# Retention and mixture kernel on one core: GpSimd's two products cut into halves, and the first batch begun in another order

## Chip, cores and metric

The kernel runs on one core of one Trainium2 chip. The metric is the device time of one execution in microseconds (us); lower is better. Of the core's engines, TensorE (PE) multiplies matrices, VectorE (DVE), ScalarE (ACT) and GpSimd (POOL) work element by element, SyncE (SP) issues most of the transfers from memory. PEld in a view is PE's loading of weights.

## What is computed

Three steps follow each other, for 8 batches of 576 rows. Cut to what matters:

```python
# 1: retention with a decay per head, no softmax; q, k, v: 8 batches, 8 heads, 576 rows, 64 wide
x = ((q @ k.T / 8) * gamma ** (i - j), lower triangle) @ v
# 2: four attention experts, two picked for each row by a gate
logits = x @ w_gate
out = sum over picked experts e of weight * softmax(causal(x@wq[e] @ (x@wk[e]).T / 8)) @ (x@wv[e]) @ wo[e]
# 3: phases, mixing over the rows (tokens), a channel product
theta = x @ w_theta; y = w_tok_r @ (x*cos(theta)) + w_tok_i @ (x*sin(theta)); u = x + y
return u + relu(u @ w_ch)
```

## The kernel before, in words

Retention goes through each batch in five chunks of 128 rows, the last one of 64 (`ROWS`). A chunk is `n` = 2 halves of 64 rows (the last chunk has one). For a chunk c, `loads` (L113) brings `kt` (queries and keys, 512 KB) and `kv` (keys and values in row order, 512 KB) through SP, and has POOL make `vp` (L122), the values scaled by the decay `gam`. `ret_scores` (L137) are 16 products for `sm`; `ret_state` (L153) adds one half's keys times `vp` to a running sum `pS` and ACT copies it to a tile `S` (L156); `ret_values` (L166, L173) sums `sm` times `vp` and `S` times queries in `px`, DVE scales that by `gt` to `xt` (L183), ACT rounds it to `xh` (L185), and POOL takes the remainder `xl` (L186). `ret_step(b, c, next)` interleaves on PE the second state of chunk c, the scores of the next chunk and the values of chunk c, and ends with the next chunk's first state.

A product with rounded and remainder parts is three matmuls: `xh` by `WH`, `xl` by `WH`, `xh` by `WL` (`mm3`, L101 to L103). `WH` and `WL` are made from the loaded weights `wst` by `split` (ACT L106, DVE L107). `proj_v` (L249, 12 matmuls, "v0" to "v4" in `work`) projects one chunk, and takes its four products with `xh` and `WH`, four with `xh` and `WL`, four with `xl` last; `proj_qk` ("k00", "q00", "k01") projects rows 0 to 287 or 288 to 575, 12 matmuls with `mm3`. A projected key is copied by four DMAs, `KK<-KN` (L227). `at_scores` (L311) begins the attention of a batch.

The order on PE is the order of the code (`manual_schedule`), that on the other engines a scheduler's, which may put POOL's `vp` of a later chunk ahead of an `xl`; each engine and each queue then runs strictly in that order. The tiles `kt` and `kv` have three buffers each (`LDB`), `vp` three (`VPB`): `ret_values` of chunk c calls `loads` for the chunk three further on, whose transfer waits until the buffer is free. SP issues no transfer while an earlier one in its list waits.

The program begins with 50 matmuls on a zeroed tile (`WARM`, L393), the loads of chunks 0 and 1, `g0` (from which DVE makes `gt`, L408), the four tiles of `w1`, and chunk 2. For batch 0 the code then goes `ret_step` 0, `ret_step` 1 (between the splits of the weights), v0, `ret_step` 2, v1, `ret_step` 3, v2, k00, `ret_step` 4, q00, v3, k01, v4: the projection of a chunk stands one `ret_step` behind it. From batch 1 on the same steps are spread over the attention units of the batch before (`SLOTS`). After all attention the token and channel products of step 3 follow, where POOL has little to do.

Of the kernel before, what the change touches and what calls it, by code (L numbers as in the profile page):

```python
# [10 lines left out]
F32 = mybir.dt.float32  # L11
# [9 lines left out]
B, H, S, D = 8, 8, 576, 64  # L21
E, DM = 4, 512
C = 128
NCH = 5
ROWS = [128, 128, 128, 128, 64]
# [11 lines left out]
LDB = 3  # L37
# [8 lines left out]
         ("v0", "R3"), ("v1", ""), ("v2 k00", "R4"), ("q00", "R5"), ("v3 k01 v4 g", "")]  # L46
PTV = (0,)
WARM = 50
WB = 7
JOBS = (58, 75)  # L50

# [10 lines left out]
def tile_kernel(ctx: ExitStack, tc: tile.TileContext, qk, kv, w1, wo, wot, wd, cst, out):  # L62
    nc = tc.nc
    consts = ctx.enter_context(tc.tile_pool(name="consts", bufs=1))

    def pool(name, **kw):
        return tc.alloc_tile_pool(name=name, bufs=1, **kw)
# [13 lines left out]
    ps1 = pool("ps1", space=PSUM)  # L81
# [4 lines left out]
    tri = att.tile([128, 64], F32, name="tri")  # L86
    gam = att.tile([128, NCH, 2, 4], F32, name="gam")
# [7 lines left out]
    gt = ret.tile([128, 4, S], F32, name="gt")  # L95
# [14 lines left out]
    MARK = {}  # L110
    QKT, KVT, XT, PSS, VP, SM, PX = {}, {}, {}, {}, {}, {}, {}

    def loads(b, c):  # L113
        R = ROWS[c]
        o = c * 1024
        t = ret.tile([128, 8, R], F32, name="kt", bufs=LDB, padded_shape=[128, 8, 128])
        nc.sync.dma_start(t, qk[b, :, o:o + 8 * R].rearrange("p (h r) -> p h r", h=8))
        n = R // 64
        u = ret.tile([128, 2, 2, 256], F32, name="kv", bufs=LDB)
        nc.sync.dma_start(u[:, :n], kv[b, c, :, :n * 512].rearrange("r (j a d) -> r j a d", j=n, a=2))  # L120
        vp = ret.tile([128, 2, 4, D], F32, name="vp", bufs=VPB)
        MARK["pool"] = nc.gpsimd.tensor_mul(vp[:, :n], u[:, :n, 1, :].rearrange("p j (h d) -> p j h d", h=4),  # L122
                                            gam[:, c, :n, :, None].to_broadcast([128, n, 4, D]))
        QKT[b, c], KVT[b, c], VP[b, c] = t, u, vp

    def half(x):
        return slice(x * 64, x * 64 + 64)

    def ret_scores(b, c):

        n = ROWS[c] // 64
        t = QKT[b, c]
        ps = ps1.tile([128, n, 4, 64], F32, name="w", bufs=WB, padded_shape=[128, 2, 4, 64])
        for j in range(n):
# [9 lines left out]
    def ret_state(b, k):  # L144

        c, j = divmod(k, 2)
        u, vp = KVT[b, c], VP[b, c]
        if k == 0:
            PSS[b] = ps1.tile([128, 4, D], F32, name="pS", bufs=1, padded_shape=[128, 4, 128])
        pS = PSS[b]  # L150
        for x in range(4):
            for s in range(2):
                nc.tensor.matmul(pS[half(s), x, :], u[half(s), j, 0, x * D:x * D + D], vp[half(s), j, x, :],  # L153
                                 start=k == 0 and x == 0, stop=False, skip_group_check=True)
            yield
        nc.scalar.activation(SB[(k + 1) % 4], pS, AF.Copy)  # L156

    def ret_values(b, c):

        R = ROWS[c]  # L160
        t, vp, sm = QKT[b, c], VP[b, c], SM.pop((b, c))
        px = ps1.tile([128, 4, R], F32, name="w", bufs=WB, padded_shape=[128, 4, 128])
        for j in range(R // 64):
            for x in range(4):
                for s in range(2):
                    nc.tensor.matmul(px[half(1 - s), x, half(j)], vp[half(s), j, x, :], sm[half(s), j, x, :],  # L166
                                     start=j == 0 and x == 0, stop=False, skip_group_check=True)
                yield
        for j in range(R // 64):
            k = 2 * c + j  # L170
            for x in range(4 if k else 0):
                for s in range(2):
                    nc.tensor.matmul(px[half(1 - s), x, half(j)], SB[k % 4][half(s), x, :], t[half(s), x, half(j)],  # L173
                                     start=False, stop=False, skip_group_check=True)
                yield
        for x in (QKT, KVT, VP):
            x.pop((b, c))
        cs = slice(c * C, c * C + R)
        if c == 0:
            XT[b] = (w1p.tile([128, 4, S], F32R, name="xh", bufs=1),  # L180
                     w1p.tile([128, 4, S], F32R, name="xl", bufs=1))
        xt = ret.tile([128, 4, R], F32, name="xt", bufs=2, padded_shape=[128, 4, 128])
        nc.vector.tensor_mul(xt, px, gt[:, :, cs])  # L183
        xh, xl = XT[b]
        nc.scalar.activation(xh[:, :, cs], xt, AF.Copy)  # L185
        nc.gpsimd.tensor_sub(xl[:, :, cs], xt, xh[:, :, cs])  # L186
        nx = (b, c + LDB) if c + LDB < NCH else (b + 1, c + LDB - NCH)
        if nx[0] < B:
            loads(*nx)

    def ret_step(b, c, nx, mid=None):

        diag, off = [], []
        if 0 <= c < NCH - 1:
            diag.append(ret_state(b, 2 * c + 1))
        if nx:
            diag.append(ret_scores(*nx))
        if c >= 0:
            off.append(ret_values(b, c))
        last = nx and nx[1] < NCH - 1  # L200
        off = chain(*off)
        for _, _ in zip_longest(chain(*diag), islice(off, 12) if last and mid else off):
            pass
        if mid:
            mid()
        for _ in zip_longest(ret_state(nx[0], 2 * nx[1]) if last else (), off):
            pass
# [4 lines left out]
    def proj_qk(b, p, t, g):  # L212
# [6 lines left out]
        sl = slice(g * HS, g * HS + HS)  # L219
        ps = ps1.tile([128, HS], F32, name="w", bufs=WB, padded_shape=[128, 512])  # L220
        for kt in range(4):
# [15 lines left out]
    def proj_v(b, c):  # L237
# [7 lines left out]
        cs = slice(c * C, c * C + R)  # L245
        ps = ps1.tile([128, NV], F32, name="w", bufs=WB, padded_shape=[128, 512])
        for x, W in ((xh, WH), (xh, WL), (xl, WH)):
# [32 lines left out]
    def work(b, names):  # L280
        for n in names.split():
            x = b + n.islower()
            if x < B:
                if n in "Gg":
                    gate(x)
                elif n[0] == "T":
                    token_tile(ps1, 0, len(X2))
                elif n[0] == "F":
                    fuse(int(n[1]))
                elif n[0] in "Vv":  # L290
                    proj_v(x, int(n[1]))
                else:
                    proj_qk(x, int(n[1]), int(n[0] in "Kk"), int(n[2]))
# [4 lines left out]
    def at_scores(u):  # L298
# [8 lines left out]
        for i, (j0, j1) in enumerate(parts):  # L307
            ps = [ps1.tile([128, j1 - j0], F32, name="w", bufs=WB, padded_shape=[128, 512]) for _ in range(2)]
            for s in range(2):
# [34 lines left out]
    def at_trans(u):  # L344
# [8 lines left out]
        for s in range(2):  # L353
            PT = PTB[b, p, g][s]
            tp = ps1.tile([128, m + 1, R], F32, name="w", bufs=WB, padded_shape=[128, 4, 128] if R == 128 else [128, 8, 64])
            for j in range(m + 1):
# [31 lines left out]
    w1s = pool("w1s")  # L388
    warm = w1s.tile([128, 128], BF, name="warm")
    nc.vector.memset(warm, 0.0)  # L390
    pw = ps1.tile([128, 128], F32, name="w", bufs=WB, padded_shape=[128, 512])
    for _ in range(WARM):
        nc.tensor.matmul(pw, warm, warm, start=True, stop=True)  # L393
    o = 320
    nc.sync.dma_start(gam, cst[:, o:o + NCH * H].rearrange("p (c j h) -> p c j h", c=NCH, j=2))
    for l in LG:
        nc.gpsimd.memset(l, 0.0)
    for x in SUM + NW:
        nc.gpsimd.memset(x, 1.0)
    loads(0, 0)  # L400
    nc.sync.dma_start(tri, cst[:, 256:320])
    loads(0, 1)
    o += NCH * H
    g0 = w1s.tile([128, 4, 128 + NCH], F32, name="g0")
    nc.sync.dma_start(g0, cst[:, o + 1088 + E * E:].rearrange("p (a t) -> p a t", a=4))
    def make_gt(c):
        R = ROWS[c]
        nc.vector.tensor_mul(gt[:, :, c * C:c * C + R], g0[:, :, :R], g0[:, :, 128 + c, None].to_broadcast([128, 4, R]))  # L408
# [8 lines left out]
    def split_w1(kt):  # L417
        split(WH[:, kt, :], WL[:, kt, :], wst[kt])

    for kt in range(4):  # L420
        load_w1(kt)
    for c in range(2, LDB):
        loads(0, c)
    with tc.issue_after(MARK["pool"].ins):
        nc.gpsimd.dma_start(cm, cst[:, o:o + 1088])
    nc.sync.dma_start(tie, cst[:, o + 1088:o + 1088 + E * E].rearrange("p (a b) -> p a b", a=E))
# [65 lines left out]
    def fuse(p):  # L492
# [2 lines left out]
            mm3(acc, wt[:, 0, p, :], wt[:, 1, p, :], th[:, 0, :], th[:, 1, :], kt == 0, kt == 3)  # L495
        split(MH[:, p, :], ML[:, p, :], acc)

    ret_step(0, -1, (0, 0))
    make_gt(0)
    ret_step(0, 0, (0, 1))  # L500
    make_gt(1)
    for kt in range(4):
        split_w1(kt)
        if kt == 1:
            ret_step(0, 1, (0, 2))
    for c in range(2, NCH):
        make_gt(c)
    w1s.release()
    work(-1, "v0")
    ret_step(0, 2, (0, 3))  # L510
    work(-1, "v1")
    ret_step(0, 3, (0, 4))
    work(-1, "v2 k00")
    ret_step(0, 4, (1, 0))
    work(-1, "q00 v3 k01 v4 g")


    X2, NR, OL = {}, {}, {}
# [84 lines left out]
    for t in range(nu + 1):  # L603
        b, k = divmod(t, 10)
        if b < B - 1:
            more, between, after = *SLOTS[k], ""
        else:
            b = B - 1
# [20 lines left out]
        if b < B - 1:  # L629
            if between[:1] == "R":  # L630
                c = int(between[1])
                x = b + 1
                def mid():
                    for o in outs:
                        at_out(*o)
                    outs.clear()
# [11 lines left out]
        x = t - JOBS[0] if i else t - 2  # L648
# [251 lines left out]
```

## Time and profile before

| what | value |
|---|---|
| median of 3 runs | 901.79 us (897.53 to 903.82) |
| the profiled execution's own time | 901.38 us |
| its span (first to last instruction) | 899.6 us |
| PE busy | 864.2 us (96%) |
| DVE, ACT, POOL busy | 614.8, 466.0, 219.2 us |
| data moved | 130.29 MB, mean 145 GB/s |

The span is that of one execution on the profiled chip; 1.8 us of the execution's time lie around it. A busy PE is not a PE at its full rate: the table counts a matmul's whole passage, and the clock that it was granted is another column. Times in the views count from the span's start.

### The profile page before, as it was taken

The numbers are of one execution on the slowest core, as the hardware profiler recorded it, in microseconds if no ns is written. First come the engines' busy times: TensorE is split into PE (matmuls) and PEld (weight loads), VectorE is DVE, ScalarE is ACT, GpSimd is POOL, SyncE is SP. The second block draws the span as 40 slices with busy tenths as digits, with TensorE's granted clock in tenths as the row PEclk, the third lists the DMA queues.
The fourth block names the chain that finished last, engine by engine and source line by source line (L and its number), as shares of the span: only waits on it lengthen the run. The fifth ranks groups of instructions, "written<-read, shape, count | busy, mean of one in ns | idle before, by whom it ended". The sixth has DMA issues, their size and how long they took to land.

```text
span 899.6 us, 25474 instructions
## 1 busy us (share of the span) xinstructions
PE 864.2 (96%) x10062; PEld 804.5 (89%) x10062; DVE 614.8 (68%) x1708; ACT 466.0 (52%) x1270; POOL 219.2 (24%) x268
## 2 busy tenths in 40 slices
PE   6998999999899999999999899999999999999998
PEld 5997888889888988988878899999999999999998
DVE  4276677878788786777768947866568764776622
ACT  2375666666666665666657613543345533445320
POOL 3434262551634435252210112000120101201010
PEclk8999999999999999999999989999999999999999
DMA  8757666676666667657795242333525124251311
GB/s 295 212 155 223 152 210 171 182 244 182 189 186 210 202 188 229 164 144 213 181 322 174 33 128 57 65 86 87 136 50 129 38 70 113 36 129 26 83 47 54
DMA packets 146215, 130.29 MB, mean 145 GB/s; under 512 B 83504, under 2 KB 121648, under 8 KB 146096
## 3 DMA queue, kind: packets, MB, share of 16 engines
q1 hardware_dynamic: 145952, 128.39, 51.1%
q8 instruction: 79, 1.29, 0.6%
q0 software_dynamic: 144, 0.28, 0.2%
q14 instruction: 40, 0.33, 0.1%
HBM read 78.03 MB, written 32.00 MB: 122 GB/s over the span
## 4 chain that ended last, share of the span: by engine, by line
PE 78%; DMA 8%; DVE 6%; POOL 3%; ACT 2%; issue 2%; SPq 1%; POOLq 0%; ACTq 0%; DVEq 0%
PE acc L725 22%; PE w L102 10%; PE w L101 10%; PE w L103 9%; DMA kv<-kv 5%; PE w L311 5%; PE w L377 4%; PE w L249 4%; PE w L358 4%; PE pS L153 2%; PE w L725 2%; PE w L137 1%; POOL xl L186 1%; PE w L173 1%; PE acc L101 1%
## 5 line engine op out<-in xcount | busy, mean ns | idle before, releaser
L725 PE MATMUL acc<-TK,zh 128*128 128x288 f32 (+2 forms) x896 | 155.8, 296 | 0.5 <-ACT ob L381 0.5
L725 PEld LDWEIGHTS acc<-TK,zh 128*128 128x128 f32 x896 | 131.9, 189 | 0.8 <-issue 0.6
L319 ACT ACTIVATE P<-P,st 128x128 f32<-128x128 f32 (+4 forms) x160 | 95.6, 598 | 44.0 <-DVE st L314 43.7
L725 PE MATMUL acc<-TK,zl 128*128 128x288 f32 (+1 forms) x448 | 95.8, 295 | 0.0
L741 POOL TENSOR_TENSOR ul<-u,uh 128x576 fp32r<-128x576 f32 x16 | 24.3, 1533 | 285.0 <-ACT uh L740 284.9
L314 DVE CUSTOM_DVE_ANT_0 P<-w,cm 128x128 f32<-128x128 f32 (+4 forms) x160 | 71.9, 476 | 10.7 <-PE w L311 10.3
L102 PE MATMUL w<-xl,WH 128*128 128x288 f32 x256 | 75.9, 296 | 2.9 <-POOL xl L186 2.9
L311 PE MATMUL w<-KK,U 128*64 128x288 f32 (+4 forms) x384 | 76.4, 327 | 0.7 <-DMA KK<-KN 0.7
L101 PE MATMUL w<-xh,WH 128*128 128x288 f32 x256 | 76.1, 297 | 0.6 <-issue 0.6
L103 PE MATMUL w<-xh,WL 128*128 128x288 f32 x256 | 75.4, 295 | 0.0
L725 PEld LDWEIGHTS acc<-TK,zl 128*128 128x128 f32 x448 | 72.3, 189 | 0.0
L106 ACT ACTIVATE zh<-cs 128x512 fp32r<-128x512 f32 x64 | 40.3, 630 | 59.7 <-PE acc L725 42.7
L107 DVE TENSOR_TENSOR zl<-cs,zh 128x512 fp32r<-128x512 f32 x64 | 44.1, 689 | 37.6 <-ACT zh L106 37.0
L576 ACT ACTIVATE cs<-cs,quarter 128x256 f32<-128x256 f32 x72 | 36.4, 506 | 60.1 <-DVE cs L574 57.2
L377 PE MATMUL w<-PT,V 128*64 128x192 f32 (+3 forms) x576 | 56.6, 325 | 6.8 <-DVE PT L363 6.3
L579 DVE SCALAR_TENSOR_TENSOR cs<-cs,x 128x512 f32<-128x512 f32 x72 | 49.3, 687 | 19.6 <-ACT cs L577 18.8
L449 POOL TENSOR_TENSOR r<-r,ex 128x192 f32<-128x192 f32 (+1 forms) x51 | 29.5, 578 | 133.3 <-ACT hl L450 57.2
L311 PEld LDWEIGHTS w<-KK,U 128*128 128x128 f32 (+1 forms) x384 | 54.1, 171 | 6.9 <-issue 2.1
L358 PE MATMUL w<-ident,P 128*128 128x128 f32 (+2 forms) x480 | 58.8, 257 | 0.0
L153 PE MATMUL pS<-vp,kv 64*64 64x64 f32 x1024 | 45.9, 227 | 12.7 <-ACT S L156 9.6
L377 PEld LDWEIGHTS w<-PT,V 128*64 128x64 f32 (+1 forms) x576 | 36.3, 135 | 24.0 <-DVE PT L363 7.1
L122 POOL TENSOR_TENSOR vp<-kv,gam 128x512 f32<-128x512 f32 (+1 forms) x40 | 38.6, 966 | 74.0 <-DMA kv<-kv 59.7
(160 smaller groups left out, 2415.1 us busy)
## 6 DMA issues: line engine op xcount, KB each, us to landing
KK<-KN SPq DMA_DIRECT2D x128, 144.0 KB
kt<-qk SPq DMA_DIRECT2D x32, 512.0 KB
kv<-kv SPq DMA_DIRECT2D x32, 512.0 KB
raw<-wd SPq DMA_DIRECT2D x43, 192.0 KB
xd<-xb SPq DMA_DIRECT2D x126, 64.0 KB
out<-u SPq DMA_DIRECT2D x28, 288.0 KB
u<-xd SPq DMA_DIRECT2D x28, 288.0 KB
td<-hl SPq DMA_DIRECT2D x27, 192.0 KB
```

The costliest lines, as they stand in the source:

```text
L101: nc.tensor.matmul(ps, ah, bh, start=first, stop=False)
L102: nc.tensor.matmul(ps, ah, bl, start=False, stop=False)
L103: nc.tensor.matmul(ps, al, bh, start=False, stop=last)
L107: nc.vector.tensor_sub(l, src, h)
L153: nc.tensor.matmul(pS[half(s), x, :], u[half(s), j, 0, x * D:x * D + D], vp[half(s), j, x, :], start=k == 0 and x == 0, stop=False, skip_g ...
L311: nc.tensor.matmul(ps[s][:R], U[:, s, rs], KK[:, s, x, j0:j1], start=x == 0, stop=x == 1)
L314: MARK["dve"] = nc.vector.tensor_tensor_reduce(Ps[s][:R, j0:j1], ps[s][:R], cm[:R, o + j0:o + j1], 1.0, st[:R, 0, s:s + 1] if i else 3.0e3 ...
L319: MARK["act"] = nc.scalar.activation(Ps[s][:R, :n], Ps[s][:R, :n], AF.Exp, bias=st[:R, last, s:s + 1], scale=-1.0, accum_out=SUM[p][:R, m, ...
L358: nc.tensor.transpose(tp[:w, j, :], Ps[s][:R, j * C:j * C + w], ident[:R, :R])
L377: nc.tensor.matmul(po[s * 64:s * 64 + 64, c0:], V[:ROWS[j], j, 2 * p + s, :], v, start=j == 0, stop=j == last, skip_group_check=True)
L579: nc.vector.scalar_tensor_tensor(z, cs, -1.0, x2[:, None, ds].to_broadcast([128, 2, 256]), op0=OP.mult, op1=OP.mult)
L725: nc.tensor.matmul(acc[d][j], A[:, dc], TK[:, kt, W, t0:t1], start=q == 0 and n == 0, stop=q == 8 and n == 2)
```

## The change

Two things. First, POOL's `vp` is made by one instruction for each half of 64 rows, and `xl` by one instruction for each two of the four slices of the model's width, everywhere. Second, the beginning: `g0` and then chunk 0 alone are loaded ahead of the weights, chunks 1 and 2 after them; the `vp` of later chunks of batch 0 is made where the code says (`scale_v`) and no longer within `loads`; all of `gt` is made first; `ret_step` 0 computes no scores of chunk 1; the weights are split after chunk 0's `xt`; 40 more matmuls on the zeroed tile follow (`WARM2`), then v0; and from there each projection stands directly behind its own chunk: scores and state of chunk 1, `ret_step` 1, v1, `ret_step` 2, v2, k00, `ret_step` 3, q00, v3, `ret_step` 4, k01, v4.

```diff
-    def loads(b, c):
+    def loads(b, c, late=False):
...
+        QKT[b, c], KVT[b, c] = t, u
+        if not late:
+            scale_v(b, c)
+
+    def scale_v(b, c):
+        n, u = ROWS[c] // 64, KVT[b, c]
         vp = ret.tile([128, 2, 4, D], F32, name="vp", bufs=VPB)
-        MARK["pool"] = nc.gpsimd.tensor_mul(vp[:, :n], u[:, :n, 1, :].rearrange("p j (h d) -> p j h d", h=4),
-                                            gam[:, c, :n, :, None].to_broadcast([128, n, 4, D]))
-        QKT[b, c], KVT[b, c], VP[b, c] = t, u, vp
+        for j in range(n):
+            MARK["pool"] = nc.gpsimd.tensor_mul(vp[:, j], u[:, j, 1, :].rearrange("p (h d) -> p h d", h=4),
+                                                gam[:, c, j, :, None].to_broadcast([128, 4, D]))
+        VP[b, c] = vp
...
-        nc.gpsimd.tensor_sub(xl[:, :, cs], xt, xh[:, :, cs])
+        for x in (slice(0, 2), slice(2, 4)):
+            MARK["xl"] = nc.gpsimd.tensor_sub(xl[:, x, cs], xt[:, x], xh[:, x, cs])
         nx = (b, c + LDB) if c + LDB < NCH else (b + 1, c + LDB - NCH)
         if nx[0] < B:
-            loads(*nx)
+            loads(*nx, not nx[0])
...
-    loads(0, 0)
-    nc.sync.dma_start(tri, cst[:, 256:320])
-    loads(0, 1)
     o += NCH * H
     g0 = w1s.tile([128, 4, 128 + NCH], F32, name="g0")
     nc.sync.dma_start(g0, cst[:, o + 1088 + E * E:].rearrange("p (a t) -> p a t", a=4))
+    loads(0, 0)
+    nc.sync.dma_start(tri, cst[:, 256:320])
...
-    for c in range(2, LDB):
-        loads(0, c)
+    for c in range(1, LDB):
+        loads(0, c, True)
...
+    for c in range(NCH):
+        make_gt(c)
     ret_step(0, -1, (0, 0))
-    make_gt(0)
-    ret_step(0, 0, (0, 1))
-    make_gt(1)
-    for kt in range(4):
-        split_w1(kt)
-        if kt == 1:
-            ret_step(0, 1, (0, 2))
-    for c in range(2, NCH):
-        make_gt(c)
+    ret_step(0, 0, None)
+    with tc.issue_after(MARK["xt"].ins):
+        for kt in range(4):
+            split_w1(kt)
+    warm_up(WARM2)
+    scale_v(0, 1)
     w1s.release()
     work(-1, "v0")
+    ret_step(0, -1, (0, 1))
+    scale_v(0, 2)
+    ret_step(0, 1, (0, 2))
+    with tc.issue_after(MARK["xl"].ins):
+        scale_v(0, 3)
+    work(-1, "v1")
     ret_step(0, 2, (0, 3))
-    work(-1, "v1")
+    with tc.issue_after(MARK["xl"].ins):
+        scale_v(0, 4)
+    work(-1, "v2 k00")
     ret_step(0, 3, (0, 4))
-    work(-1, "v2 k00")
+    work(-1, "q00 v3")
     ret_step(0, 4, (1, 0))
-    work(-1, "q00 v3 k01 v4 g")
+    work(-1, "k01 v4 g")
```

The order on three engines at the beginning, before and after the change; the numbers tell buffers and tiles of one name apart. On ACT, the first instructions before the change (`xt_321` is chunk 0's `xt`, `xt_405` chunk 1's, `w_433` the sum of v0):

```order
L156 ACTIVATE S1_136<-pS_256 128x256
L106 ACTIVATE WH_132<-wst_221 128x772
L156 ACTIVATE S2_137<-pS_256 128x256
L106 ACTIVATE WH_132<-wst_223 128x772
L106 ACTIVATE WH_132<-wst_225 128x772
L156 ACTIVATE S3_138<-pS_256 128x256
L106 ACTIVATE WH_132<-wst_227 128x772
L185 ACTIVATE xh_319<-xt_321 128x4x128
L156 ACTIVATE S0_135<-pS_256 128x256
L156 ACTIVATE S1_136<-pS_256 128x256
L185 ACTIVATE xh_319<-xt_405 128x4x128
L252 COPY V_432<-w_433 128x256
```

And on ACT after the change (`xt_304` is chunk 0's, `w_367` the sum of v0):

```order
L107 ACTIVATE WH_132<-wst_216 128x772
L164 ACTIVATE S1_136<-pS_258 128x256
L107 ACTIVATE WH_132<-wst_218 128x772
L107 ACTIVATE WH_132<-wst_220 128x772
L164 ACTIVATE S2_137<-pS_258 128x256
L107 ACTIVATE WH_132<-wst_222 128x772
L193 ACTIVATE xh_302<-xt_304 128x4x128
L261 COPY V_366<-w_367 128x256
```

The first copy of the state (`S1`) now stands behind the first weight tile's rounding, and v0 follows chunk 0's `xh` at once, where chunk 1's `xh` stood between.

On POOL before the change, the instructions of chunks 2, 3 and 4 of batch 0 (`xl` from `xt_508`, `xt_594`, `xt_676`) and the `vp` of batch 1's chunks 0, 1 and 2 (from `kv_514`, `kv_600`, `kv_682`):

```order
L122 TENSOR_TENSOR vp_413<-kv_411,gam_123 128x256
L122 TENSOR_TENSOR vp_516<-kv_514,gam_123 128x512
L186 TENSOR_TENSOR xl_320<-xt_508,xh_319 128x4x128
L122 TENSOR_TENSOR vp_602<-kv_600,gam_123 128x512
L186 TENSOR_TENSOR xl_320<-xt_594,xh_319 128x4x128
L122 TENSOR_TENSOR vp_684<-kv_682,gam_123 128x512
L186 TENSOR_TENSOR xl_320<-xt_676,xh_319 128x4x64
```

And after (chunks 2, 3, 4: `xt_568`, `xt_680`, `xt_759`; batch 1: `kv_575`, `kv_687`, `kv_766`):

```order
L130 TENSOR_TENSOR vp_577<-kv_575,gam_123 128x256 x2
L195 TENSOR_TENSOR xl_303<-xt_568,xh_302 128x2x128 x2
L130 TENSOR_TENSOR vp_589<-kv_479,gam_123 128x256
L130 TENSOR_TENSOR vp_689<-kv_687,gam_123 128x256 x2
L195 TENSOR_TENSOR xl_303<-xt_680,xh_302 128x2x128 x2
L130 TENSOR_TENSOR vp_768<-kv_766,gam_123 128x256 x2
L195 TENSOR_TENSOR xl_303<-xt_759,xh_302 128x2x64 x2
```

In both, one `vp` of batch 1 stands ahead of each `xl`; every full instruction has become a pair.

On SP's list before, the loads of that stretch (`kv_514`, `kv_600`, `kv_682` as above; `KK_620<-KN_621` are the copies of k00's key):

```order
L120 DMA kv_514<-kv 128x1024
L433 DMA raw_1042<-wd 128x384
L120 DMA kv_600<-kv 128x1024
L117 DMA kt_512<-qk 128x1024
L433 DMA raw_1182<-wd 128x384
L120 DMA kv_682<-kv 128x1024
L117 DMA kt_598<-qk 128x1024
L227 DMA KK_620<-KN_621 64x2x288 x4
L117 DMA kt_680<-qk 128x1024
```

And after (`kv_575`, `kv_687`, `kv_766` as above):

```order
L121 DMA kv_575<-kv 128x1024
L118 DMA kt_573<-qk 128x1024
L121 DMA kv_687<-kv 128x1024
L236 DMA KK_607<-KN_608 64x2x288 x4
L118 DMA kt_685<-qk 128x1024
L121 DMA kv_766<-kv 128x1024
L118 DMA kt_764<-qk 128x1024
```

Batch 1's third `kv` has moved from ahead of the four copies of k00's key to behind them and behind one `kt`.

## Rows read from the trace of the kernel before

**Rows 1.** The page's first part: busy us, share of the span, instructions.

```profile
PE 864.2 (96%) x10062; PEld 804.5 (89%) x10062; DVE 614.8 (68%) x1708; ACT 466.0 (52%) x1270; POOL 219.2 (24%) x268
```

**Rows 2.** Stretches: length; PE, PEld, DVE, ACT, POOL busy; granted clock; DMA share; GB/s.

```profile
10.00:15.00 5.00, 1.03 (x40) 0.78 (x32) 4.10 (x6) 2.71 (x5) 1.04 (x1) 0.91 1.03 410
15.00:20.00 5.00, 4.16 (x112) 3.78 (x112) 4.58 (x8) 1.90 (x4) 2.67 (x2) 0.50 0.82 312
```

**Rows 3.** Chain that ended last, 24 to 44 us: start, us, what.

```profile
24.67 0.20 PE pS L153 x2
...
26.98 0.51 issue
...
29.40 0.20 PE pS L153 x2
...
31.42 1.64 PE w L249 x12
...
33.86 0.55 issue
...
35.46 0.20 PE w L137 x2
...
37.01 0.33 PE w L101
...
41.80 1.43 PE w L249 x12
```

**Rows 4.** Timeline of PE: start, us, instruction, count, idle before and releaser.

```profile
1.03 4.28 PE L393 MATMUL w<-warm 128*128 128x128 bf16 x50 [1.03 <-DVE warm L390]
...
5.24 1.15 PE L137 MATMUL w<-kt 64*64 64x64 f32 x32
...
13.10 0.68 PE L153 MATMUL pS<-vp,kv 64*64 64x64 f32 x16 [2.75 <-ACT S L156]
```

**Rows 5.** Timeline of DVE, then of ACT.

```profile
10.90 2.75 DVE L408 TENSOR_TENSOR gt<-g 128x512 f32<-128x512 f32 x4 [3.60 <-DMA g<-cst]
...
16.52 1.82 DVE L107 TENSOR_TENSOR WL<-wst,WH 128x772 fp32r<-128x772 f32 x2
...
26.87 0.68 DVE L183 TENSOR_TENSOR xt<-w,gt 128x512 f32<-128x512 f32 x1
...
11.88 0.85 ACT L106 ACTIVATE WH<-wst 128x772 fp32r<-128x772 f32 x1 [3.21 <-DMA wst<-w]
12.63 0.36 ACT L156 ACTIVATE S<-pS 128x256 f32<-128x256 f32 x1
...
28.14 0.62 ACT L185 ACTIVATE xh<-xt 128x512 fp32r<-128x512 f32 x1
```

**Rows 6.** Timeline of POOL.

```profile
6.46 1.04 POOL L122 TENSOR_TENSOR vp<-kv,gam 128x512 f32<-128x512 f32 x1 [5.36 <-DMA kv<-kv]
...
17.34 2.47 POOL L186 TENSOR_TENSOR xl<-xt,xh 128x512 fp32r<-128x512 f32 x1 [6.04 <-ACT xh L185]
...
29.20 1.04 POOL L122 TENSOR_TENSOR vp<-kv,gam 128x512 f32<-128x512 f32 x1 [3.27 <-DMA kv<-kv]
...
38.14 0.73 POOL L186 TENSOR_TENSOR xl<-xt,xh 128x256 fp32r<-128x256 f32 x1 [0.84 <-ACT xh L185]
...
66.00 0.61 POOL L122 TENSOR_TENSOR vp<-kv,gam 128x256 f32<-128x256 f32 x1 [0.89 <-DMA kv<-kv]
```

**Rows 7.** Timeline of SP's queue: issues.

```profile
20.25 5.45 SPq L120 DMA_DIRECT2D kv<-kv  x2
...
36.43 2.73 SPq L227 DMA_DIRECT2D KK<-KN  x4
```

**Rows 8.** Chain that ended last, 61 us: a load on it.

```profile
61.38 4.49 DMA kv<-kv
```

**Rows 9.** Waits of PE over the whole span: us in total, times, longest.

```profile
PE w L102 <- POOL xl L186: 2.9, 5, 1.1
PE w L249 <- POOL xl L186: 2.5, 2, 2.4
```

More of the change, by code (lines that the diff above doesn't have):

```diff
@@ L48 @@
 WARM = 50
+WARM2 = 40
 WB = 7
@@ L182, in ret_values @@
         xt = ret.tile([128, 4, R], F32, name="xt", bufs=2, padded_shape=[128, 4, 128])
-        nc.vector.tensor_mul(xt, px, gt[:, :, cs])
+        MARK["xt"] = nc.vector.tensor_mul(xt, px, gt[:, :, cs])
         xh, xl = XT[b]
         nc.scalar.activation(xh[:, :, cs], xt, AF.Copy)
-        nc.gpsimd.tensor_sub(xl[:, :, cs], xt, xh[:, :, cs])
+        for x in (slice(0, 2), slice(2, 4)):
+            MARK["xl"] = nc.gpsimd.tensor_sub(xl[:, x, cs], xt[:, x], xh[:, x, cs])
         nx = (b, c + LDB) if c + LDB < NCH else (b + 1, c + LDB - NCH)
         if nx[0] < B:
-            loads(*nx)
+            loads(*nx, not nx[0])
     def ret_step(b, c, nx, mid=None):
@@ L390, in tile_kernel, with warm_up @@
     nc.vector.memset(warm, 0.0)
-    pw = ps1.tile([128, 128], F32, name="w", bufs=WB, padded_shape=[128, 512])
-    for _ in range(WARM):
-        nc.tensor.matmul(pw, warm, warm, start=True, stop=True)
+    def warm_up(n):
+        pw = ps1.tile([128, 128], F32, name="w", bufs=WB, padded_shape=[128, 512])
+        for _ in range(n):
+            nc.tensor.matmul(pw, warm, warm, start=True, stop=True)
+    warm_up(WARM)
     o = 320
```

## The prediction

> **What bounds the kernel.** I read the busy shares first, then PE's waits, then the chain that ended last. The span is 899.6 us by the table, and the profiled execution took 901.38 us, 0.4 below the median of the runs (901.79); my sum is made against 901.38. PE sets the pace: it is busy 864.2 us, 96% of the span [rows 1], so only what leaves it idle, or slows its clock, can be won or lost. The change touches two places. One is POOL's work, for which PE waits at L102 and L249 for 2.9 and 2.5 us over the whole run [rows 9], part of it in the beginning. The other is the beginning up to the first attention scores, which stand at 43.23 us (v4 starts at 41.80 and takes 1.43) [rows 3]. There PE idles: 1.03 us busy between 10 and 15 us, and after that its clock is granted at 0.50, the lower level of 1.2 GHz, with 4.16 us busy from 15 to 20 [rows 2]. v0, the step of chunk 1 and the first state of chunk 2 are done at 24.67 us [rows 3]. From there on PE works with small pauses, because each projection stands a step behind its chunk.
>
> **The beginning, until the same work is done.** Two loads of 512 KB no longer stand ahead of the weights. At 410 GB/s [rows 2] these 1.05 MB take 2.6 us, so the first weight tile, rounded from 11.88 on when it had landed [rows 5], comes at 9.3, and the others 1.0 us apart (395 kB each at that rate): 10.3, 11.2, 12.2. g0 (272 kB) goes ahead of chunk 0, which costs 0.7: scores at 5.9 instead of 5.24 [rows 4], kv at 7.1 instead of 6.46 [rows 6]. The scores take 1.15, gt cannot be late (g0 lands no later than the larger kt did, 5.24; four gt take 2.75 [rows 5], the short one under 0.7, done by 8.7, and sm after it is not yet waited for). The first half of vp is there at 7.1 + 0.61 [rows 6], the state's products follow, but then S1 stands on ACT behind the first weight tile: 9.3 + 0.85 + 0.36 [rows 5] = 10.5. PE's next state waits for that; before, it waited for no weight here. The rest of chunk 0 is 32 products; a step with 40 took 1.55 (35.46 to 37.01 [rows 3]), so 1.3, to 11.8. xt takes 0.68, to 12.5, and DVE then makes four WL at 0.91 each [rows 5], to 16.2. ACT has its last WH at 13.05 and xh at 13.7. xl runs beside WL; there the whole of it took 2.47 [rows 6], so both halves end at 16.2 too, and v0's last matmuls at about 16.8. The 40 matmuls take 40 x 0.086 = 3.4 us [rows 4], from 11.8 to 15.2: hidden under WL, free here. Without that cover they would cost at most these 3.4.
>
> After v0 come chunk 1's scores (1.15), its state (0.68), S (0.36) and its step (24.67 to 26.98, 2.3 [rows 3]): 4.5 us. The work that was done at 24.67 is now done at 21.3. **Gain 3.4 us**; between 2.4 (weights 1 us later, since cm now shares the queues) and 4.4 (S1 not delayed).
>
> **What is lost behind it.** The rest took 18.56 us before (24.67 to 43.23), with two issue pauses of 0.51 and 0.55 [rows 3] in it. Now each projection waits for its own chunk.
>
> v1: values end some 0.3 before the step does; xt 0.68, xh 0.62 [rows 5] and about 0.15 of hand-overs come next, so PE stands 1.1; with the second half of xl a little more. 1.2.
>
> v2: the same 1.1, and more. On POOL the vp of batch 1's chunk 0 stands ahead of chunk 2's xl, and its kv can only be loaded when the buffer is free, some 0.7 into step 2. Before, that load's issue ended at 25.70 [rows 7] and vp began at 29.20 [rows 6], 4.5 after the step's beginning at 24.67. Then come two halves of vp (1.22) and two of xl (0.73 each [rows 6]), 7.3 in all, and two matmuls, 0.3; without any wait v2 would end 2.3 + 1.64 after the step's beginning. That is 3.6, and 3.4 is taken, since no weight data (raw) shares the queue this time; with a load 0.7 faster 2.9.
>
> v3: q00 covers most of it, 0.2.
>
> k01: it needs chunk 4's xl, ahead of which stands the vp of batch 1's chunk 2, whose kv now stands on SP behind the four copies of k00's key and one kt. From k00's end: 0.97 until the first copy is issued (35.46 to 36.43), 2.73 for the four [rows 3, 7], 0.68 for one more issue, a load of 4.5 (the row on the chain [rows 8]; 3.8 by the quieter one above), vp 1.22, half of a short xl 0.45 (between half of the 0.73 and all of it): 10.6. PE has meanwhile steps 3 (29.40 to 31.42) and 4 (1.55), q00 (1.6) and v3 (1.43), the 0.2 above and one matmul: 6.9. So 3.7 of waiting; I take 3.4, and 2.9 with the quick load, over 5 with a slower one.
>
> Together 1.2 + 3.4 + 0.2 + 3.4 = 8.2, of which the two issue pauses (1.06) fall inside: 7.1. Against the gain of 3.4 this leaves **3.7 us more** at the first scores. After them PE is dense and its order unchanged, so the shift stays.
>
> **The halves, in the rest of the run.** A pair costs 2 x 0.61 against 1.04 for vp [rows 6], 0.18 more; 2 x 0.73 for xl is dearer than a whole one by about as much. The GPSIMD Engine Reference of the Trainium skill (Performance versus the Vector engine) gives such an operation a cost by element, 4497 ns for 2048; by that two halves of 256 would cost as much as one of 512, about 1.12, and the change nothing. The rows show a fixed part, and the rows are what I use. POOL is busy 24% of the span [rows 1], so this hides, except on the chain kv, vp, xl, PE. There the first half of xl comes 2.31 - 1.95 = 0.36 earlier, but the second 0.37 later; v takes its xl part as two and two matmuls of 0.14, so it ends where it did; k01 needs the second half six matmuls later, and gains some 0.1 to 0.4 at each of five waits. I take 0; bounds are 1 us less, and 1 us more where a pair delays the next load.
>
> Sum: 901.4 + 3.7 = **905.1**.
>
> **Rivals.** (a) The loads are there in time, and only xt and xh are waited for: v1 1.2, v2 1.2, v3 0.2, k01 1.3, together 3.9; less 1.06 and less the gain 3.4: 900.8. Against it stands POOL's order, with the vp ahead of each xl, and the wait of 3.27 for that kv [rows 6]. (b) PE's clock falls in the new pauses. Before, it fell behind the stretch from 10 to 15 us in which PE was busy 1.03 us, and stayed at half from 15 to 20 with 4.16 us busy, half of which, 2.1, a full clock would have saved [rows 2]. Around v2 and at k01 PE stands 3 to 4 us with little between. One such fall costs 2 us: 907.2. TensorE: Matmul & The Clock Gate (What's actually happening), in the Trainium skill, has the clock halve for an array left idle and return with steady work; the fall before agrees. By that rule each of the two pauses counts. The side beyond 1%: the clock falls at both, each time for two such stretches (2 x 4.2), 913.5; it decides only if PE stays as sparse behind k01, which the dense projections speak against. (c) The halves take away all of PE's waits for POOL, 5.4 us [rows 9], and the loads are in time: 900.8 - 5.4 = 895.4. Against it: half of xl is no use to a matmul that waits for the load ahead of it. (d) The change of order does nothing: the gain is eaten by S1 and WL alone and the pauses are as before, 901.4. The transfer of 1.05 MB ahead of the weights speaks against it.
>
> **Chances.** The forecast (903 to 906.5) 0.45; (a) and (d), 899 to 903, 0.25; (b) with one fall 0.16, with two for long 0.04; (c) 0.05; outside all, 0.05. The range reaches from (a) to the forecast with one slow load or one fall: 899.0 to 909.0. Faster by over 1% (under 892.8), which is about what a measurement of this kernel can tell from no change, needs more than all of PE's idle time at the beginning: 0.02. Slower by over 1% (over 910.8) needs (b) twice: 0.05. Within 1%: 0.93.
>
> **What would show it.** Right: v0 done near 16.8, with WL and not the weights' landing or the 40 matmuls as its last releaser; PE waiting for xl at v2 and k01 for 2 us or more each, with vp waiting for a DMA just before; first scores at 46 to 48 us; from there the profile as before. Wrong: v0 done after 19, or PE waiting on xh alone, or the first scores before 43; or a clock of half in any stretch behind 20 us, which is rival (b).

## The result and the profile after

| | before | after |
|---|---|---|
| median of 4 runs each | 902.81 us (897.53 to 905.78) | 913.13 us (912.34 to 916.42) |
| ratio | | 1.0138, 95% interval 1.0109 to 1.0168 |
| profiled execution, its span | 901.38, 899.6 us | 913.87, 912.1 us |
| first attention scores, on the chain of waits | 43.23 us [rows 3] | 57.91 us |

The changed kernel is slower by 10 us, where 3.7 was forecast. The page's busy line after the change (the one of [rows 1]), and PE's waits for what is new on its list, over the whole span (us in total, times, longest):

```profile
PE 873.9 (96%) x10102; PEld 811.7 (89%) x10102; DVE 615.3 (67%) x1708; ACT 467.0 (51%) x1270; POOL 232.7 (26%) x340
```

```profile
PE w L103 <- POOL xl L195: 5.6, 5, 2.8
...
PE w L258 <- POOL xl L195: 4.2, 6, 2.8
...
PE w L258 <- ACT xh L193: 2.5, 2, 1.3
```

PE's waits for `xl`, 5.4 us before [rows 9], became 9.8, the longest 2.8 at both lines. All of the loss stands in the first 58 us: the first scores come 14.7 us later than before, and the shift is 13.3 at PE's last instruction and 12.5 at the span's end. PE's timeline of the beginning (start, us, instruction, idle before it and its releaser; L258 is the matmul of v0 to v4, L102 and L103 the first two of k01, L320 the first scores, which stands 0.2 us ahead of its place on the chain because matmuls overlap in this view; the lines stand 1 to 19 lower in the code than before):

```profile
17.71 0.39 PE L258 MATMUL w<-WL,xh 128*128 128x260 f32 x1 [1.02 <-DVE WL L108]
19.00 0.39 PE L258 MATMUL w<-WL,xh 128*128 128x260 f32 x1 [0.90 <-DVE WL L108]
19.22 0.64 PE L258 MATMUL w<-WH,xl 128*128 128x260 f32 x4
26.86 0.74 PE L258 MATMUL w<-WH,xh 128*128 128x260 f32 x4 [1.27 <-ACT xh L193]
32.47 0.75 PE L258 MATMUL w<-WH,xh 128*128 128x260 f32 x4 [1.28 <-ACT xh L193]
36.49 1.49 PE L258 MATMUL w<-WH,xl 128*128 128x260 f32 x4 [2.80 <-POOL xl L195]
49.11 0.40 PE L102 MATMUL w<-xh,WH 128*128 128x288 f32 x1 [1.10 <-ACT xh L193]
52.30 0.61 PE L103 MATMUL w<-xl,WH 128*128 128x288 f32 x1 [2.79 <-POOL xl L195]
57.70 0.70 PE L320 MATMUL w<-KK,U 128*128 128x128 f32 x4
```

v0 ends at 19.86 (19.22 + 0.64), not at 16.8. The pause ahead of v1 begins at 25.59, which is where the same work is done as before at 24.67. Then come the pauses: 1.27 at v1, 1.28 and 2.80 at v2, 1.10 and 2.79 at k01. The stretches after (length; PE, PEld, DVE, ACT, POOL busy; granted clock; DMA share; GB/s), as in [rows 2]:

```profile
10.00:15.00 5.00, 4.63 (x94) 4.54 (x95) 1.74 (x3) 3.45 (x6) 0.30 (x1) 0.66 1.05 376
15.00:20.00 5.00, 3.08 (x32) 2.44 (x31) 3.94 (x3) 0.10 (x1) 5.00 (x6) 1.00 1.04 387
20.00:25.00 5.00, 4.43 (x158) 4.27 (x158) 0.84 (x2) 1.12 (x4) 0.56 (x1) 0.66 0.15 46
...
35.00:40.00 5.00, 3.51 (x14) 3.33 (x15) 0.00 (x0) 0.45 (x2) 2.69 (x5) 0.50 0.16 57
...
50.00:55.00 5.00, 2.70 (x11) 2.71 (x12) 0.00 (x0) 0.00 (x0) 2.01 (x4) 0.62 0.27 99
55.00:60.00 5.00, 5.00 (x31) 4.98 (x30) 1.98 (x12) 1.79 (x8) 0.00 (x0) 0.70 0.45 106
```

In its first 500 us the kernel before was at half clock once, from 14.0 to 24.3 us; the same view of it (the stretch 15 to 20 is in [rows 2]):

```profile
20.00:25.00 5.00, 4.14 (x52) 3.89 (x56) 0.47 (x1) 1.19 (x4) 3.38 (x4) 0.57 0.74 159
25.00:30.00 5.00, 4.49 (x173) 4.15 (x168) 1.29 (x2) 1.89 (x7) 1.73 (x3) 1.00 0.72 238
```

In the changed kernel the clock is at half from 10.2 to 13.6 and from 20.4 to 23.9, and again around v2 and k00, from 34.1 to 40.9, and around k01 and v4, from 51.2 to 58.0. (The ends of these stretches come from the same view in steps of 0.5 us.) DVE and ACT are nearly idle around v2 and k01, and the chain of waits shows what is being waited for (start, us, what):

```profile
29.56 4.85 DMA kv<-kv
...
35.14 0.61 POOL vp L130
35.75 0.69 POOL xl L195
...
36.49 1.49 PE w L258 x4
37.98 0.24 PE w L102
...
45.94 4.55 DMA kv<-kv
...
50.65 1.18 POOL vp L130 x2
51.83 0.42 POOL xl L195
...
52.30 0.61 PE w L103
...
55.30 2.60 PE w L258 x12
57.91 0.50 PE w L320 x4
```

From 29.56 to 52.30 the chain is: a load of batch 1, its `vp`, `xl` behind it, v2, k00 (each matmul 0.24 us; at the full clock it is 0.13), the copies of k00's key on SP, the next load of batch 1, `vp`, `xl`, k01. Two loads that batch 1 does not need yet decide when batch 0 goes on.

### The profile page after: what moved, and what is told of

It is laid out like the page before. It is cut to its first block, busy times and chain, and to the rows that moved or that the text cites. A ratio compares the mean times of both kernels' runs of the same rounds, so it can differ in the third digit from the quotient of the medians.

```text
span 912.1 us, 25630 instructions
## 1 busy us (share of the span) xinstructions
PE 873.9 (96%) x10102; PEld 811.7 (89%) x10102; DVE 615.3 (67%) x1708; ACT 467.0 (51%) x1270; POOL 232.7 (26%) x340
## 4 chain that ended last, share of the span: by engine, by line
PE 72%; DMA 8%; DVE 6%; POOL 4%; SPq 3%; ACT 3%; issue 3%; POOLq 0%; ACTq 0%; DVEq 0%
PE acc L744 20%; PE w L103 9%; PE w L104 9%; PE w L102 9%; DMA kv<-kv 6%; PE w L320 4%; PE w L258 4%; PE w L386 4%; PE w L367 3%; SPq L236 2%; PE pS L161 2%; POOL xl L195 2%; POOL vp L130 2%; PE w L744 2%; PE acc L102 1%
## 5 line engine op out<-in xcount | busy, mean ns | idle before, releaser
L760 POOL TENSOR_TENSOR ul<-u,uh 128x576 fp32r<-128x576 f32 x16 | 24.3, 1535 | 285.2 <-ACT uh L759 285.2
L103 PE MATMUL w<-xl,WH 128*128 128x288 f32 x256 | 77.1, 301 | 5.6 <-POOL xl L195 5.6
L102 PE MATMUL w<-xh,WH 128*128 128x288 f32 x256 | 77.1, 301 | 1.1 <-ACT xh L193 1.1
L320 PE MATMUL w<-KK,U 128*64 128x288 f32 (+4 forms) x384 | 76.6, 328 | 0.5 <-ACT ob L390 0.5
L130 POOL TENSOR_TENSOR vp<-kv,gam 128x256 f32<-128x256 f32 x72 | 44.5, 637 | 80.3 <-DMA kv<-kv 60.9
L195 POOL TENSOR_TENSOR xl<-xt,xh 128x256 fp32r<-128x256 f32 (+1 forms) x80 | 55.7, 717 | 23.5 <-ACT xh L193 23.5
L320 PEld LDWEIGHTS w<-KK,U 128*128 128x128 f32 (+1 forms) x384 | 54.1, 172 | 6.9 <-issue 2.1
```

Of the source, the lines that this page charges most:

```text
L102: nc.tensor.matmul(ps, ah, bh, start=first, stop=False)
L103: nc.tensor.matmul(ps, ah, bl, start=False, stop=False)
L130: MARK["pool"] = nc.gpsimd.tensor_mul(vp[:, j], u[:, j, 1, :].rearrange("p (h d) -> p h d", h=4), gam[:, c, j, :, None].to_broadcast([128, ...
L195: MARK["xl"] = nc.gpsimd.tensor_sub(xl[:, x, cs], xt[:, x], xh[:, x, cs])
L320: nc.tensor.matmul(ps[s][:R], U[:, s, rs], KK[:, s, x, j0:j1], start=x == 0, stop=x == 1)
```

## The experiments

Each time is a median. The kernel before ran beside each group of them, at 901.33 us (e1 to e4), 900.35 (e5 to e8), 902.51 (e9, e10) and 899.58 (e11, e12), so the ratios to it are what is compared. Where an expectation names the time of a copy of V or of a change of the clock, it stands 0.25 us later than the views have it; the text below goes by the views.

**Which half of the change.** First the halves alone, in the kernel before:

```diff
+        for j in range(n):
+            MARK["pool"] = nc.gpsimd.tensor_mul(vp[:, j], ...)
...
+        for x in (slice(0, 2), slice(2, 4)):
+            nc.gpsimd.tensor_sub(xl[:, x, cs], xt[:, x], xh[:, x, cs])
```

> The kernel before with the first half of the change alone: POOL's vp and xl in two instructions each, the beginning as it was. Theory A (the whole loss of 10.3 us is made in the new beginning, the halves are worth nothing): no change, 902.8, between 901.3 and 904.3. Theory B (the halves cost: each pair holds POOL longer and delays PE some 0.1 us at each of the 80 pairs): 908 or more. Rival C of the prediction, halves take PE's waits for POOL away: below 900.

Measured: 903.99 us, ratio 1.0037 (1.0004 to 1.0070). And the new beginning alone, the changed kernel with `vp[:, :n]` and `xl[:, :, cs]` whole again:

> The changed kernel with whole vp and xl again, so the new beginning alone. Theory A: 913, between 911 and 915, since half of an xl is no use where both halves stand behind the same vp. Theory B: 905 or less. A third way: the halves help only in the new beginning, where PE stands for xl, and this run is slower than the changed kernel by over 2 us, 915 to 917.

Measured: 913.55, ratio 1.0137 (1.0094 to 1.0180); the changed kernel had 1.0138. So the beginning is the loss, and the halves neither help it nor cost more than a few tenths of a per cent. The 13.5 us by which POOL is busier thus lie mostly beside other work.

**Which part of the beginning.** The loads and v0 stay, each later projection goes one step behind its chunk again:

```diff
-    work(-1, "v1")
     ret_step(0, 2, (0, 3))
...
-    work(-1, "v2 k00")
+    work(-1, "v1")
     ret_step(0, 3, (0, 4))
-    work(-1, "q00 v3")
+    work(-1, "v2 k00")
     ret_step(0, 4, (1, 0))
-    work(-1, "k01 v4 g")
+    work(-1, "q00 v3 k01 v4 g")
```

> The changed kernel with its loads, its v0 and its halves, but v1, v2, v3 and k01, v4 one step behind their chunk again, as before the change. Theory A (the pauses at v1, v2 and k01, and the half clock that follows two of them, are the loss): the work that the kernel before had done at 24.7 us is done at 25.6, the rest goes as before, so 902.8 + 0.9 = 903.7, between 902 and 905, and no half clock behind 30 us. Theory L (it is the order of the loads: with weights first, the loads of the later chunks and of batch 1 come late whatever PE's order): 909 or more, with PE waiting for loads or for POOL's vp between 30 and 55 us.

Measured: 903.73, ratio 1.0023 (0.9998 to 1.0048), and no half clock between 15.2 and 97 us. One pause for `xl` was left in its trace:

```profile
43.48 0.40 PE L103 MATMUL w<-xl,WH 128*128 128x288 f32 x1 [2.15 <-POOL xl L195]
```

The order of the loads is thus not the loss; the projections that stand directly behind their chunks are. The next kernel keeps them there, and changes POOL's order alone:

```diff
-            loads(*nx, not nx[0])
+            loads(*nx, nx[0] < 2 and not b)
+        if nx[0] == 1 and not b:
+            with tc.issue_after(MARK["xl"].ins):
+                scale_v(*nx)
```

> The changed kernel with one thing different: on POOL the xl of chunks 2, 3 and 4 of batch 0 stands ahead of the vp of batch 1, not behind it. The changed kernel's two pauses of 2.80 and 2.79 us for xl should shrink to about 0.9 and 0.5, which is 4.2 us less. Theory A1 (the clock falls because of these two long pauses): the two stretches of half clock, 34.3 to 41.2 and 51.4 to 58.2, go too; PE worked 4.7 and 5.9 us in them, of which a full clock saves half, 5.3 us; together 913.1 - 9.5 = 903.6, between 902 and 906. Theory A2 (the clock falls anyway, from the 1.2 us pauses for xh and the sparse work): 913.1 - 4.2 = 908.9, with the two half stretches still there. Theory L (late loads only move the wait to another place): 912 or more.

Measured: 905.66, ratio 1.0049 (1.0024 to 1.0073), and the clock in its stretches (views as above):

```profile
35.00:40.00 5.00, 5.00 (x120) 4.80 (x118) 1.67 (x4) 2.24 (x5) 1.29 (x3) 1.00 0.64 185
...
50.00:55.00 5.00, 5.00 (x40) 4.97 (x39) 3.68 (x15) 3.39 (x12) 0.00 (x0) 1.00 0.43 95
```

Both long pauses are gone, the three of 1.1 to 1.3 us for `xh` are still there, and with them alone the clock of this trace stays at its full level from 16.4 us on, past 500. The saving, 0.89% or 8 us, is more than the two pauses could give (4.2 expected) and near the 9.5 expected for pauses and clock: theory A1.

**The clock alone.** The pauses stay, but PE multiplies the zeroed tile in them:

```diff
+        if (b, p, t, g) == (0, 0, 1, 1):
+            warm_up(44)
...
+            if x is xl and (b, c) == (0, 2):
+                warm_up(30)
```

> The changed kernel, with matmuls on the zeroed tile put into its two long pauses and nothing else moved: 30 ahead of v2's part with xl, 44 ahead of k01. They compute nothing that is used; at 0.086 us each (50 took 4.28) they fill 2.6 and 3.8 us, no longer than PE stood there (2.80; 1.10 + 2.79 with one matmul between). So the waits for xl end when they ended, and only PE's work before it changes. Theory A1 (what PE does around a pause decides its clock, and the half clock is a loss of its own): no half clock behind 30 us, and of 4.7 and 5.9 us worked at half a half comes back, 5.3 us less: 907.8, between 906 and 909.5. Theory A2 (the half clock hides nothing that counts, since PE would wait for xl, for the loads of batch 1 or for KK anyway): 912 to 914.

Measured: 909.64 (just over the 909.5 that theory A1 allowed), ratio 1.0089 (1.0058 to 1.0119), 0.49% or 4.4 us under the changed kernel, only just clear of the noise of the two ratios. The traces show where it is won, with the clock at its full level where it had been halved (stretches, then v2's `xl` part, then the chain from k01 on):

```profile
35.00:40.00 5.00, 3.70 (x72) 3.15 (x73) 0.19 (x1) 0.86 (x3) 2.76 (x5) 1.00 0.21 57
...
50.00:55.00 5.00, 4.14 (x33) 4.14 (x34) 0.94 (x6) 0.89 (x4) 1.22 (x3) 1.00 0.06 16
```

```profile
36.55 0.51 PE L262 MATMUL w<-WH,xl 128*128 128x260 f32 x2 [1.12 <-POOL xl L195]
```

```profile
50.86 0.40 PE w L103
...
52.58 1.43 PE w L262 x12
54.01 0.40 PE w L324 x4
```

This kernel does more work on PE and is faster. v2's `xl` part begins at 36.55, as late as without the filling (36.49), so the two traces are level there. From there k01's `xl` comes 1.4 us sooner (50.86 against 52.30), and k01 and v4 then take 3.15 us in place of 5.61, 2.5 less; the first scores stand at 54.01 in place of 57.91. So the half clock behind a pause is a loss of its own, here 3.9 us for the two.

**v0's end.** On top of e4_xl_first, three WL go ahead of chunk 0's `xt`:

```diff
+    for kt in range(3):
+        split_w1(kt)
     ret_step(0, 0, None)
     with tc.issue_after(MARK["xt"].ins):
-        for kt in range(4):
-            split_w1(kt)
+        split_w1(3)
```

> The kernel with xl first (e4_xl_first), and on DVE the first three WL made ahead of chunk 0's xt, while DVE stands idle for over 3 us and POOL is idle too; in the changed kernel all four stand behind xt, beside POOL's xl and vp, and took 0.95, 1.51, 1.48 and 1.37 us. Theory E (a DVE product of two tiles and a POOL product exclude each other for their whole length, and this moved v0's end from the 16.8 us predicted to 19.9): WL 0.95 each, v0's copy at 20.50 before comes at 17.8 to 18.6, and the time falls by about 2 to 903.6, between 902 and 905. Theory F (the weights' landing, not DVE, sets v0's end): the copy stays within 0.5 of 20.5 and the time at 905.7.

Measured: 909.77, ratio 1.0089 (1.0060 to 1.0119): no faster, which was a miss of the time. v0's copy came at 17.08, even 3.2 us sooner than in e4_xl_first (20.25); 1.1 of this was there before the WL counted, since `xt` began at 12.49 against 13.61, with a shorter stretch of half clock ahead of it. DVE's and POOL's timelines, first of the changed kernel, then of this one:

```profile
13.86 5.08 DVE L108 TENSOR_TENSOR WL<-wst,WH 128x772 fp32r<-128x772 f32 x4
...
14.70 2.13 POOL L195 TENSOR_TENSOR xl<-xt,xh 128x256 fp32r<-128x256 f32 x2 [4.72 <-ACT xh L193]
16.80 3.76 POOL L130 TENSOR_TENSOR vp<-kv,gam 128x256 f32<-128x256 f32 x4
```

```profile
9.65 2.93 DVE L108 TENSOR_TENSOR WL<-wst,WH 128x772 fp32r<-128x772 f32 x3 [1.01 <-ACT WH L107]
...
13.09 0.95 DVE L108 TENSOR_TENSOR WL<-wst,WH 128x772 fp32r<-128x772 f32 x1
...
13.93 1.41 POOL L195 TENSOR_TENSOR xl<-xt,xh 128x256 fp32r<-128x256 f32 x2 [4.29 <-ACT xh L193]
15.30 1.18 POOL L130 TENSOR_TENSOR vp<-kv,gam 128x256 f32<-128x256 f32 x2
```

Apart, four WL take 3.9 us and a pair of `xl` 1.41; side by side 5.08 and 2.13. Theory E holds for v0. But v1's copy came only 0.3 us sooner than in e4_xl_first (27.73 against 28.05), after a wait of PE's own (next part) and a stretch of half clock from 24.6 to 28.0. That the runs are slower still (904 to 915, the traced one 904.9) was not settled.

**PE's waits without a releaser.** All repairs together, the loads of the changed kernel, three WL early, projections one step behind, `xl` first in batch 0:

> All three repairs in one, with the halves kept: the loads of the changed kernel, three WL ahead of xt, each projection one step behind its chunk as before the change, and xl ahead of batch 1's vp on POOL. By the sums so far v4's copy stands at 46.9 with the step behind alone; less 2.15 for the wait for xl at k01 and 2.2 for v0 this is 42.6, against 43.5 before the change. So 0.9 less than before, and the halves' own small cost (0 to 3): 900.4 to 903.5; a gain over the kernel before that these rounds can tell would be under 899. No half clock between 20 and 60 us.

Measured: 902.99, ratio 1.0024 (0.9999 to 1.0048), within the expected times, near their upper end. But the clock was at half from 24.8 to 28.2, where none was expected. The same with whole `vp` and `xl`:

> The same as e7_behind_xl_wl with whole vp and xl. If halves cost something for themselves (e1_halves_only stood 0.4% over the kernel before, barely outside what its rounds can tell), this is 1 to 3 us under e7_behind_xl_wl and at or under the kernel before: 898 to 901. If they cost nothing, the two agree within 1.5 us.

Measured: 904.20, ratio 1.0040 (1.0019 to 1.0061): the halves cost nothing here. Part of what the early v0 wins goes in waits that the view calls "issue". PE's timeline of e7_behind_xl_wl, then of a kernel that has `WARM2 = 8` in place of 40:

```profile
22.73 0.27 PE L181 MATMUL w<-kt,S 64*64 64x64 f32 x1 [1.82 <-issue]
```

```profile
22.52 0.50 PE L161 MATMUL pS<-vp,kv 64*64 64x64 f32 x10 [2.28 <-issue]
```

> The same as e7_behind_xl_wl with 8 matmuls on the zeroed tile ahead of v0 instead of 40, which is 64 instructions of PE fewer (each has a weight load). It asks what PE's waits of 1.1 to 1.9 us with no releaser in the views are, which stood in e7_behind_xl_wl at 22.73, on the first product of a stored state S with chunk 1's queries. Theory G (PE's code comes in pieces of 256 instructions: all such waits so far stand at PE's 706th, 962nd or 1218th instruction, about 1.4 us after a 16 KB packet of an instruction queue has landed): the wait stays at the 706th instruction, and so moves 64 instructions later in the work, to another product, still 1.2 to 1.6 us behind the end of such a packet. Theory H (it is a wait for data that the views don't name, S or the queries): it stays at that product of a state with queries, now PE's 642nd instruction. The time itself is expected within 3 us of e7_behind_xl_wl either way.

One run: 904.07 us. The wait stays at PE's 706th instruction and moves from L181 to L161: theory G. The table has the starts from the timelines, and the packets from the traces; PE's instructions are counted with the weight loads and the few of its sequencer:

| kernel | at PE's instruction | packet of 16 KB ends, us | PE goes on, us |
|---|---|---|---|
| before | 962, 1218 | 26.03, 33.00 | 27.50, 34.41 |
| e3_step_behind | 962 | 26.69 | 28.16 |
| e6_wl_early | 706 | 20.93 | 22.34 |
| e7_behind_xl_wl | 706 | 21.20 | 22.73 |
| e8_whole | 706, 962 | 20.12, 24.27 | 21.46, 25.72 |
| e9_fewer_records | 706, 962, 1218 | 21.12, 26.13, 32.17 | 22.52, 27.54, 33.36 |

**POOL's order everywhere.** In the kernel before, too, a `vp` stands ahead of each `xl`:

```diff
+        with ExitStack() as es:
+            if "xl" in MARK:
+                es.enter_context(tc.issue_after(MARK["xl"].ins))
             MARK["pool"] = nc.gpsimd.tensor_mul(vp[:, :n], ...)
```

> The kernel before with one thing different, in all batches: on POOL each xl stands ahead of the next vp and not behind it; no halves, the beginning as it was. The trace of the kernel before shows PE waiting for POOL's xl 5.4 us in all, 2.38 of it in one wait at 76.5 us behind a vp whose load was late. Theory P (the order on POOL is what makes xl late, in every batch as in the new beginning): most of the 5.4 goes, and 3 to 5 us are won: 895.5 to 898, about 0.4% under the kernel before. Theory Q (vp moved behind xl is late for the next state's products, and PE waits there instead): no gain, 899 to 903.

Measured: **894.00 us, ratio 0.9899 (0.9866 to 0.9932)**, faster than both kernels. PE's longest groups of waits (as in [rows 9]) no longer hold `xl`:

```profile
PE pS L156 <- ACT S L159: 7.8, 10, 1.7
PE w L380 <- DVE PT L366: 4.7, 9, 1.9
PE pS L156 <- issue: 3.7, 2, 2.6
```

The gain is larger than the 5.4 us of waits; by the copies of V in the two traces the kernel is 0.8 us ahead at v4, 3.7 at 95 us and 9.0 at 363, and 6.4 at the end. PE's busy time is the same in both traces (864.2 and 864.3), so all that the traced execution won, 6.6 us of its span, is idle time: besides the waits for `xl`, other waits of PE grew and shrank, which was not taken apart further. The same edit in the changed kernel, and in e8_whole:

> The changed kernel with xl ahead of the next vp on POOL in all batches, and nothing else undone: the halves and the new beginning stay. In batch 0 alone this order took the changed kernel from 913.1 to 905.7 (e4_xl_first); in the kernel before, in all batches, it gave 8 us (e10_before_xl_first), most of it from batch 1 on. Theory P (the POOL order is one cause in both places and the gains add up): 905.7 less some 6 to 8, so 898 to 900, still 4 to 6 over e10_before_xl_first, which is what the new beginning costs without its POOL waits. Theory R (with xl first the new beginning is as good as the old): 893 to 896.

> The best parts together: weights ahead of chunks 1 and 2, three WL ahead of xt, projections one step behind their chunks, whole vp and xl, and xl ahead of the next vp in all batches. With e8_whole at 904.2 and a gain of 8 from batch 1 on this gives 896; if the new beginning is as good as the old one, 894, the same as e10_before_xl_first. Under 891 it would be a gain of its own, which only a run without the waits for code and the late KK copies of e8_whole could show; not expected.

Measured: 897.92, ratio 0.9981 (0.9959 to 1.0002), and 894.01, ratio 0.9937 (0.9918 to 0.9956). The gains add up (theory P). With POOL in order the rest of the change still costs 0.8% (0.9981 against 0.9899), and its best form 0.4% or, within the intervals, nothing; it wins nothing. In e12's trace (its slowest execution, 897.32) PE still waits 1.17 and 0.81 us for its code and 1.4 for the copies of a key, and is at half clock from 24.0 to 30.8.

## Why the prediction was wrong

**The beginning, forecast as a gain of 3.4, was a loss of 0.9.** Three rows of the changed kernel (ACT, DVE, SP) that belong to this and the next point:

```profile
9.11 0.85 ACT L107 ACTIVATE WH<-wst 128x772 fp32r<-128x772 f32 x1 [7.08 <-DMA wst<-w]
...
13.26 0.69 DVE L191 TENSOR_TENSOR xt<-w,gt 128x512 f32<-128x512 f32 x1 [4.24 <-PE w L181]
...
41.83 3.42 SPq L236 DMA_DIRECT2D KK<-KN  x4
```

The weights came as reckoned, at 9.11 against 9.3. Then two steps failed. "The rest of chunk 0 is 32 products ... to 11.8" took a full clock for granted; `xt` began at 13.26, 1.5 later, since PE ran at half clock from 10.2 to 13.6. In the traces of e5 and e11, which share this beginning and had no such stretch there, `xt` began at 11.85 and 11.82, as reckoned, and v0's copy came at 18.06 and 18.05 and not at 19.90. DVE in e5:

```profile
11.85 0.69 DVE L191 TENSOR_TENSOR xt<-w,gt 128x512 f32<-128x512 f32 x1 [3.06 <-PE w L181]
```

So this part of the loss belongs to where the clock fell in the traced execution, and need not be the same in others. The second step is "DVE then makes four WL at 0.91 each ... xl runs beside WL": the four took 5.08, 1.4 more. That the two do not run side by side could be read ahead: `xl` took 2.47 us beside WL, but 0.73 for half its size alone [rows 5, 6]. There POOL alone waited and the WL kept their 0.91; the 2.47 was taken as the price of `xl`, and WL's was not raised, while here `xl` comes in two instructions and POOL's `vp`, which nothing holds back, come on top. DVE and POOL take turns. A WL that started together with the pair's first `xl` (0.72, its length alone) took 1.51 in place of 0.95, and the second `xl` then 1.44. The page "SBUF — State Buffer" of the Trainium skill (SBUF: two separate sides) states this rule, a pair of ports that the two share under an exclusive lock for a whole instruction; the trace agrees. Behind v0 the scores, the state and the step of chunk 1 took 5.7 us (19.86 to 25.59) for the 4.5 reckoned, at half clock from 20.4 to 23.9.

**The pauses were right**, in place, cause and nearly in size: v1 1.2 forecast and 1.27 measured, v2 3.4 and 4.08, k01 3.4 and 3.89, v3 0.2 and none; 8.2 and 9.24 together. The chain to k01 was forecast at 10.6 us from k00's end and took 11.4 (40.86 to 52.25); the four copies took 3.42 for the 2.73 assumed.

**Rival (b) happened, with two falls**; it had a chance of 0.16 with one fall and 0.04 with two long ones. This is the step that failed behind v0: the sum holds nothing for the clock. It was set aside because "the dense projections speak against" it; but the fall comes with the pause, and it was the dense projections behind it that ran at half: k00 at 0.24 a matmul, k01 and v4 in 5.6 us (52.30 to 57.91), where e5 took 3.15 at the full clock.

The sum of the changed kernel's own rows: 0.9 + 9.24 less the 1.06 of issue pauses is 9.1; the first scores came 14.7 later, so 5.6 are left for the slower matmuls; PE worked some 10 us in the two half stretches (36.49 to 40.9, 52.30 to 58.0), of which a full clock would save half. Against the forecast of 3.7 the first scores came some 11 us later than reckoned: 4.3 from the beginning, 1.0 from the pauses, 5.6 from here. The trace of e5 gives back 3.9 of it (4.4 by the medians), and in e4's trace, without the two long pauses, the clock does not fall. That the 913.5 named for two long falls lies so near the measured 913.13 is luck: it has 8.4 us for the clock and still a gain of 3.4 in the beginning.

"TensorE: Matmul & The Clock Gate" of the Trainium skill (What's actually happening) has the clock halve for an array left idle. In this trace it did not take the whole long pause: at v2 the clock fell at 34.1 us, when PE had stood 1.28 us, worked for 1.2 and stood another 0.4; at k01 at 51.2, when it had stood 1.10, done one matmul and stood another 1.7. One pause of 1.28 alone, in e4, was not followed by a fall.

**The halves** were forecast at 0, and e1, e2, e7 and e8 agree with that within 0.4%.

Of the signs named in advance, the pauses for `xl` behind a `vp` that waits for a load came true, and so did WL as v0's last releaser; "v0 done after 19" and "a clock of half in any stretch behind 20 us" were the two that named what went wrong.

## What to carry to other kernels

An instruction for later work that waits for a load, put ahead of one that the matrix engine waits for now, holds up everything behind it on its engine. Look at each engine's order for that first: mending it was worth 1% here with nothing else changed. Price a pause of the matrix engine with the slow clock that may follow it (here 3.9 us behind two). Count a DVE and a GpSimd product of two tiles each as one queue, not as two. Work brought forward counts only if what follows it can follow: here the next loads, the clock and the code itself were late.

## What was not expected of the hardware

PE's code arrives in pieces of 256 instructions, in packets of 16 KB of an instruction queue; the page's list of queues, the same for both kernels, has 79 packets, and 79 times 256 is 20,224, for 20,204 matmuls and weight loads of the changed kernel:

```profile
q8 instruction: 79, 1.29, 0.6%
```

Where PE's short products outrun it, PE stands until 1.2 to 1.5 us after the packet's end, in all ten cases of the table; the waits were 0.3 to 2.3 us. The trace of the changed kernel, whose data was later, has none of them in its beginning, though that of e5_filler, with the same code there, has one (1.68 us at the 706th), and e6_wl_early lost 1.7 of the 3.2 us that it had won at v0 to one. And the clock is not the same from run to run at one place. In kernels with the same order of instructions up to v0 the first half stretch ran from 10.2 to 13.6 us (the changed kernel), 11.7 to 15.1 (e3), 9.6 to 16.4 (e4) and 18.5 to 21.9 (e11), and in e5 there was none before 26.3. One trace was kept of each, so how often each happens is not known.
